# Attention products of a pair of heads: two runs for four on TensorE, and two 256-column fills in one PSUM bank

## The chip, the cores and the metric

The kernel runs on one core of one Trainium2 chip. The metric is the device time of one execution in microseconds (us). A core has five engines that work side by side, each through its own list of instructions in order: TensorE (PE, matrix products into the accumulator memory PSUM), VectorE (DVE), ScalarE (ACT), GpSimd (POOL) and SyncE (SP), which issues the transfers. One engine waits for another by semaphores that stand in front of an instruction; everything behind that instruction on the same engine waits with it. PSUM is used in banks of 512 float32 columns.

## The reference

Two results are computed from separate inputs and set side by side. The left half is attention in four segments of 512 rows with 32 heads of 18 features, with a memory that is carried from segment to segment; the right half is a two-dimensional Fourier transform written as products with given cosine and sine matrices.

```python
for s in range(N):                                   # N = 4 segments of L = 512, H = 32 heads
    qs, ks, vs = q[:, :, s], k[:, :, s], v[:, :, s]
    logits = jnp.einsum("bhqd,bhkd->bhqk", qs, ks) * scale + mask
    p = _softmax(logits, axis=-1)
    a_dot = jnp.einsum("bhqk,bhkd->bhqd", p, vs)
    ...
    outs.append(g * a_mem + (1.0 - g) * a_dot)
...
a = jnp.einsum("bsd,ed->bse", x, dft_hid_re)
b = jnp.einsum("bsd,ed->bse", x, dft_hid_im)
y = jnp.einsum("ts,bse->bte", dft_seq_re, a) - jnp.einsum("ts,bse->bte", dft_seq_im, b)
```

The sign of the mask is such that row i sees column j for j <= i, so of each 512 x 512 block of logits the kernel makes four row blocks of 128 rows with 128, 256, 384 and 512 columns.

## The kernel before

The program has three stages. From 0 to about 218 us the projections and the memory are made. From about 218 to 920 us two kinds of work share TensorE: the attention of 4 x 32 = 128 heads, and the transform, called the dense work. Behind that stands an output projection. The change lies in the middle stage.

**Dense work** (`hidden`, L620 on, and `sequence` and `product`, L642 and L580 on) is a long row of float32 products of 288 columns into the tiles `d` (L584 and L629 to L634). Each product has its own load of 128 x 128 weights (PEld in the profile), which can run beside the product ahead of it.

**Attention** (`attention`, L1155 on) runs in 68 passes, p = 0 to 67, over pairs of heads. Pass p holds steps of several pairs at once: the even head of pair p, the odd head of pair p - 2 (F_LAG = 2), the even head of pair p - 3 (T_LAG) and both heads of pair p - 4 (V_LAG). NP = 64 is the number of pairs. A pass is cut into eight slots, each ended by a `yield SLOTS[i]`. Behind each yield the main loop puts in dense work until its share has caught up with the attention's, so what stands between two yields goes to TensorE as one **run** of attention products, and dense products stand between the runs. The order on each engine is the order in which the program writes the instructions; there is no scheduler.

The steps that the change touches:

- `scores(n, kind)` multiplies queries and keys of head n into a bank tile `s` or `t` (L969). Kind 0 is the row block of 512 columns, kind 1 the blocks of 384 and 128 columns, kind 2 the block of 256 columns. `bank` hands out two `s` banks in turn, and two `t` banks.
- `smallest` (L975) adds the causal mask on DVE, writes the sum back into the bank and keeps the row minimum of the negated logits; each block is one such pass over the bank and a second, short instruction that reads the result out. DVE is free of a block only behind the second.
- `s_fill` is `scores` and `smallest` for an even head, whose minimum goes into `negm`; of it only the minimum is wanted. `f_fill` is the same for an odd head, with the minimum in `nb`; kind 0 takes a `t` bank. Its logits stay in the bank until `f_exp` (L995 and L998, on ACT) has taken their exponential into SBUF.
- `t_fill` makes the transposed logits of an even head (L1044 to L1054), `pv` the sums of probabilities and values of one head: 20 short products into the tile `pv` (L1093 and L1094). `pv_out` takes both heads' sums out on DVE. `f_turn` (L1014) is the transfer that transposes an odd head's probabilities before its `pv`; `maxima` (L1019 to L1022, POOL) splits the minima of two even heads for a later product.

Before the change a pass has four runs: A in slot 1 (`s_fill` 0, `t_fill` 0 and 1, `s_fill` 1), B in slot 3 (`pv` of the even head, `s_fill` 2), C in slot 4 (`f_fill` 1, `t_fill` 2, `f_fill` 0) and D in slot 6 (`pv` of the odd head, `f_fill` 2). In the text f1, f0, f2 stand for the products of `f_fill` 1, 0, 2 and s0, s1, s2 for those of `s_fill`.

Of the kernel before, what the change touches and what calls it, by code (L numbers as in the profile page):

```python
# [12 lines left out]
F32 = mybir.dt.float32  # L13
# [3 lines left out]
AF = mybir.ActivationFunctionType  # L17
# [5 lines left out]
S, D, H, DH, NSEG, L = 2048, 576, 32, 18, 4, 512  # L23
P = 128
# [16 lines left out]
def infini_attention_and_fnet(ctx: ExitStack, tc: tile.TileContext, xT, wqk, w8, wv, wo, beta, xtT, cT, hT, out):  # L41
    nc = tc.nc
    act, dve, pool, pe = nc.scalar, nc.vector, nc.gpsimd, nc.tensor
# [44 lines left out]
    def later(n, fn, *a):  # L88
        due.setdefault(clock[0] + n, []).append((fn, a))
# [374 lines left out]
    def stacks(p_, i):  # L464
        qs_bufs.append(p_.tile([P, 4, L], BF16, name=f"qs{i}"))
        ks_bufs.append(p_.tile([P, 4, L], BF16, name=f"ks{i}"))
        pool.memset(ks_bufs[i].bitcast(F32)[96:], BF16_ONES)
# [20 lines left out]
    def stack_load(G):  # L488
        if G < NG:
            s, g8 = divmod(G, 8)  # L490
            rows = slice(g8 * 72, g8 * 72 + 72)
            for n, (buf, src) in enumerate(((ks_bufs, kd), (qs_bufs, qd))):
                later(1 + n, dma, buf[G % 4][:NPAIR], src[s][rows].rearrange("(h d) c t -> (d c) h t", d=DH))
# [71 lines left out]
    def bank(name, shape, dtype, tag):  # L565
        turns[tag] ^= 1
        return ps.tile(shape, dtype, name=name, tag=f"{tag}{turns[tag]}", bufs=1)
# [392 lines left out]
    ROWS = (((3, 0),), ((0, 384), (2, 0)), ((1, 0),))  # L960
    FIRST_COL = {3: 0, 2: 512, 0: 896, 1: 1024}

    def scores(n, kind, tag="s"):
        G, h = divmod(n, 4)
        q, k = qs_bufs[G % 4][:NPAIR, h], ks_bufs[G % 4][:NPAIR, h]
        o = bank("s", [P, L], F32, tag)
        for i, c in ROWS[kind]:
            w = (i + 1) * P
            pe.matmul(o[:, c:c + w], q[:, i * P:w], k[:, :w], start=True, stop=True)  # L969
        return o  # L970
# [7 lines left out]
    def s_fill(n, kind):  # L978
        G, h = divmod(n, 4)
        smallest(scores(n, kind), kind, -1.0, NEGM[G % 2][:, 2 * h:2 * h + 4])  # L980
# [3 lines left out]
    def f_fill(n, kind):  # L984
        o = scores(n, kind, "s" if kind else "t")
        if kind == 1:
            F_[n] = [sa.tile([P, 4], F32, name="nb", bufs=2), sa.tile([P, 1280], F32, name="pf", bufs=3), {}]
        smallest(o, kind, -SCALE, F_[n][0])
        F_[n][2][kind] = o

    def f_exp(n, kind):
        nb, f, o = F_[n]
        o = o.pop(kind)
        m = nb[:, (slice(3, 4), slice(0, 3, 2), slice(1, 2))[kind]]
        act.activation(m, m, AF.Copy, bias=LIFT)  # L995
        for i, c in ROWS[kind]:
            w = (i + 1) * P
            act.activation(f[:, FIRST_COL[i]:FIRST_COL[i] + w], o[:, c:c + w], AF.Exp, bias=nb[:, i:i + 1], scale=-1.0)  # L998

    def f_split_hi(n):  # L1000
        f = F_[n][1]
# [14 lines left out]
    def maxima(G):  # L1016
        m, b = NEGM[G % 2].rearrange("p (h n) -> p h n", h=2), MB[G % 2][:, :24].rearrange("p (h c n) -> p c h n", h=2, c=3)
        r = sa.tile([P, 2, 4], F32, name="negx", bufs=2)
        pool.tensor_copy(b[:, 0], m)  # L1019
        pool.tensor_tensor(r, m, b[:, 0], OP.subtract)  # L1020
        pool.tensor_copy(b[:, 1], r)
        pool.tensor_tensor(b[:, 2], r, b[:, 1], OP.subtract)  # L1022

    def maxima_transpose(G, o):
        t = o[:, 384:512]
        pe.matmul(t, MB[G % 2], ident16, start=True, stop=True)
        yield
        w = sa.tile([24, P], BF16, name="mt", bufs=2)
        act.activation(w, t[:24], AF.Copy)
        for h in range(2):  # L1030
            later(1, dma, qs_bufs[G % 4][NPAIR:NPAIR + 3, 2 * h].rearrange("c (n t) -> c n t", n=4), w[12 * h:12 * h + 12])
# [64 lines left out]
    def pv_out(n2):  # L1096
        G, hh = divmod(n2, 2)
        s, g8 = divmod(G, 8)
        o = PV.pop(n2)
        og = OG[G % 2]  # L1100
        h0 = 4 * g8 + 2 * hh
        w = o[:, 440:].rearrange("p (h i c) -> p h i c", h=2, c=1)
        b = o[:, :144].rearrange("p (h i d) -> p h i d", h=2, i=4)
        o = o[:, :440].rearrange("p (h i c) -> p h i c", h=2, i=4)
        a = sa.tile([P, 8, DH], F32, name="pa", bufs=2)
        dve.reciprocal(w, o[:, :, :, 54:])
        dve.tensor_tensor(w, w, g1[:, h0:h0 + 2, None, None].to_broadcast([P, 2, 4, 1]), OP.mult)
        dve.tensor_reduce(a, o[:, :, :, :54].rearrange("p h i (c d) -> p (h i) d c", c=3), axis=AX, op=OP.add)
        to = og[:, :, 36 * hh:36 * hh + 36].rearrange("p i (h d) -> p h i d", d=DH)
        a = a.rearrange("p (h i) d -> p h i d", h=2)  # L1110
        if s == 0:
            dve.tensor_tensor(to, a, w.to_broadcast([P, 2, 4, DH]), OP.mult)
        else:
            dve.tensor_tensor(b, a, w.to_broadcast([P, 2, 4, DH]), OP.mult)
            dve.tensor_tensor(to, to, b, OP.add)
        if hh == 1:
            later(6, turn_out, G)
# [33 lines left out]
    F_LAG, T_LAG, V_LAG = 2, 3, 4  # L1151
    NP = 2 * NG
    SLOTS = (1060.0, 890.0, 1060.0, 660.0, 890.0, 1060.0, 650.0, 1210.0)

    def attention():  # L1155
        for p in range(NP + V_LAG):
            def even(lag, fn, *a):
                if 0 <= p - lag < NP:
                    fn(2 * (p - lag), *a)

            def odd(lag, fn, *a):
                if 0 <= p - lag < NP:
                    fn(2 * (p - lag) + 1, *a)

            if p < 2:
                OG.append(sa.tile([P, 4, 72], F32, name=f"og{p}"))
            if p == 0:
                stack_load(1)
                later(20, value_load, 0)
            if p % 2 == 0:  # L1170
                later(39, value_load, p // 2 + 1)
                later(30, memory_load, p // 2)
            even(T_LAG + 1, t_lo, 0)
            odd(F_LAG + 1, f_exp, 2)
            odd(F_LAG + 1, f_split_hi)
            yield SLOTS[0]
            G = p // 2 - 1 if p % 2 == 0 and 0 < p <= NP else None
            even(0, s_fill, 0)
            even(T_LAG, t_fill, 0)
            even(T_LAG, t_fill, 1, G)  # L1180
            even(0, s_fill, 1)
            if G is not None and p < T_LAG:
                list(maxima_transpose(G, bank("trm", [P, L], F32, "t")))
            odd(F_LAG + 1, f_split_lo, pool, 512, 1280)
            yield SLOTS[1]
            even(T_LAG, t_lo, 1)
            odd(F_LAG + 1, f_split_lo, dve, 0, 512)
            yield SLOTS[2]
            even(V_LAG, pv)
            if p < 2:  # L1190
                stacks(sq, p + 2)
            even(0, s_fill, 2)
            even(T_LAG, t_mask)
            yield SLOTS[3]
            odd(F_LAG, f_fill, 1)
            even(T_LAG, t_fill, 2)
            odd(F_LAG, f_fill, 0)
            if p % 2 and p < NP:
                maxima(p // 2)
            yield SLOTS[4]  # L1200
            odd(F_LAG + 1, f_turn)
            if p % 2:
                if p == 1:
                    later(6, stack_load, 2)
                else:
                    stack_load((p + 3) // 2)
                if 2 < p < 18:
                    later(2, copy_parts, 2, 7 + p // 2)
            elif 4 <= p < 36:
                later(2, copy_parts, 3, (p - 4) // 2)  # L1210
            even(T_LAG, t_hi)
            yield SLOTS[5]
            odd(V_LAG, pv)
            odd(F_LAG, f_fill, 2)
            odd(F_LAG, f_exp, 1)
            even(T_LAG, t_lo, 2)
            yield SLOTS[6]
            odd(F_LAG, f_exp, 0)
            if V_LAG <= p < NP + V_LAG - 1:
                pv_out(p - V_LAG)  # L1220
            yield SLOTS[7]
# [8 lines left out]
    for n, w in enumerate(attention()):  # L1230
        tick()
        ta += w
        for fn, a in PLAN.pop(n, ()):
            fn(*a)
        while td / total_d < ta / total_a:
            t = next(d, BREAK)
            if t is BREAK:
                break
            td += t
# [56 lines left out]
```

## Time and profile before

| what | value |
|---|---|
| median of three runs | 984.33 us (983.99 to 985.59) |
| the profiled execution's own time | 983.87 us |
| its span, first to last instruction | 982.2 us |
| TensorE products busy | 974.7 us (99%) |
| TensorE weight loads busy | 916.3 us (93%), beside the products |
| DVE, ACT, POOL busy | 746.6, 715.2, 664.4 us |
| granted TensorE clock, mean | 0.999 |

The page of the profile gives busy time by engine, and the chain of work that ended last. A timeline row gives start, duration, engine, line, operation, the tile written, the tiles read, the shape, how many equal instructions follow each other (x) and, in square brackets, idle time of the engine ahead of it with what ended it. Since products are pipelined, the recorded durations overlap; what a product costs TensorE is the distance from its start to the start of the one behind it. The first dense product behind a fill starts, in the records, some 0.03 us behind the fill's start, and the distance to the next one then holds the rest of the fill; so the cost of a run is read from its first start to the start of a dense product some places behind it, less what dense products cost there, for each dense product between.

### The profile page before, as it was taken

To read this page: it belongs to the slowest core of one execution; us is meant where nothing else is said; L and a number is where in the kernel's file an instruction comes from. 1 tells how busy PE (TensorE), PEld (TensorE's weight loads), DVE (VectorE), ACT (ScalarE), POOL (GpSimd) and SP (SyncE) were. 2 spreads that over 40 slices of the span, in tenths; PEclk is the share of its full clock that TensorE was granted. 3 is DMA by queue.
4 is the path that set the end of the run, shared out by engine and by line. 5 is a ranking of instruction groups with operands and counts; after the bars stand their busy time and mean duration, and the time that the engine had idled before them with its cause. 6 is when DMAs were issued, how large, how long until landed. Compare 5 with 4: busy or idle time off the path is not lost.

```text
span 982.2 us, 25421 instructions
## 1 busy us (share of the span) xinstructions
PE 974.7 (99%) x9246; PEld 916.3 (93%) x9246; DVE 746.6 (76%) x2113; ACT 715.2 (73%) x1687; POOL 664.4 (68%) x746
## 2 busy tenths in 40 slices
PE   9999999999999999999999999999999999999998
PEld 8989989899999999999999999999999999999998
DVE  6657668594677767777887777778888899988884
ACT  6757576664887787877878788887777877878442
POOL 2657577686667766676776776667677987776561
PEclk9999999999999999999999999999999999999999
DMA  7637557766877998999999997789999999997663
GB/s 240 200 118 242 199 171 252 238 239 182 191 183 209 219 239 233 216 210 254 233 243 241 235 210 191 184 203 217 242 238 252 242 237 240 233 207 184 173 203 109
DMA packets 304350, 209.96 MB, mean 214 GB/s; under 512 B 204992, under 2 KB 259136, under 8 KB 304192
## 3 DMA queue, kind: packets, MB, share of 16 engines
q1 hardware_dynamic: 304000, 208.20, 82.5%
q8 instruction: 72, 1.18, 0.5%
q14 instruction: 54, 0.44, 0.1%
q10 hardware_dynamic: 224, 0.14, 0.0%
HBM read 122.37 MB, written 58.98 MB: 185 GB/s over the span
## 4 chain that ended last, share of the span: by engine, by line
PE 98%; ACT 1%; DVE 1%; issue 0%
PE d L584 41%; PE s L969 7%; PE v L84 6%; PE qk L84 6%; PE qk L251 6%; PE pv L1093 4%; PE d L629 3%; PE d L630 3%; PE d L631 3%; PE t L869 2%; PE pv L1094 2%; PE d L869 2%; PE s L869 2%; PE m L364 1%; PE t L1044 1%; PE look L397 1%
## 5 line engine op out<-in xcount | busy, mean ns | idle before, releaser
L975 DVE CUSTOM_DVE_ANT_0 s<-s,causal 128x128 f32<-128x128 f32 (+3 forms) x512 | 250.1, 504 | 104.3 <-PE s L969 98.1
L457 POOL TENSOR_TENSOR clo<-craw,chi 128x512 fp32r<-128x512 f32 x159 | 217.6, 1369 | 97.1 <-ACT chi L452 72.2
L584 PE MATMUL d<-wide,chi 128*128 128x288 f32 x1408 | 260.1, 302 | 0.0
L584 PEld LDWEIGHTS d<-wide,chi 128*128 128x128 f32 x1408 | 210.5, 188 | 0.7
L584 PE MATMUL d<-wide,clo 128*128 128x288 f32 x704 | 171.2, 310 | 0.0
L1009 POOL TENSOR_TENSOR hl<-pf,hl 128x768 f16<-128x768 f32 x64 | 113.9, 1780 | 70.3 <-ACT hl L1005 56.1
L969 PE MATMUL s<-ks,qs 108*128 108x128 bf16 (+3 forms) x512 | 131.6, 301 | 1.9 <-ACT pf L998 1.8
L1057 ACT ACTIVATE phi<-t 128x384 f16<-128x384 f32 x128 | 61.7, 482 | 98.1 <-PE t L1054 98.1
L998 ACT ACTIVATE pf<-s,nb 128x128 f32<-128x128 f32 (+3 forms) x256 | 128.1, 526 | 6.2
L584 PE MATMUL d<-ab,chi 128*128 128x288 f32 x640 | 122.3, 300 | 0.0
L584 PEld LDWEIGHTS d<-wide,clo 128*128 128x128 f32 x704 | 117.7, 188 | 0.9
L452 ACT ACTIVATE chi<-craw 128x512 fp32r<-128x512 f32 x160 | 99.6, 623 | 2.8 <-DMA craw<-xtT 1.8
L584 PEld LDWEIGHTS d<-ab,chi 128*128 128x128 f32 x640 | 97.6, 188 | 0.3
L1005 ACT ACTIVATE hl<-pf 128x768 f16<-128x768 f32 (+1 forms) x128 | 87.4, 729 | 2.0
L584 PE MATMUL d<-ab,clo 128*128 128x288 f32 x320 | 82.4, 306 | 0.0
L629 PE MATMUL d<-wide,chi 128*128 128x288 f32 x256 | 79.7, 311 | 0.0
L630 PE MATMUL d<-wide,chi 128*128 128x288 f32 x256 | 75.6, 295 | 0.0
L631 PE MATMUL d<-wide,clo 128*128 128x288 f32 x256 | 75.6, 295 | 0.0
L1061 ACT ACTIVATE pf<-t 128x512 f32<-128x512 f32 (+1 forms) x128 | 68.7, 537 | 7.4 <-PE t L1044 7.3
L1076 POOL TENSOR_TENSOR plo<-pf,phi 128x384 f16<-128x384 f32 x64 | 60.7, 948 | 15.1 <-ACT pf L1061 12.6
L969 PEld LDWEIGHTS <-qs 108*128 108x128 bf16 x512 | 44.4, 97 | 16.3 <-issue 2.7
L289 POOL TENSOR_TENSOR p<-r,p 128x512 bf16<-128x512 f32 x36 | 43.4, 1206 | 22.3 <-ACT p L288 21.1
(286 smaller groups left out, 2596.6 us busy)
## 6 DMA issues: line engine op xcount, KB each, us to landing
craw<-cT SPq DMA_DIRECT2D x128, 256.0 KB
ks<-kd SPq DMA_DIRECT2D x32, 432.0 KB
qs<-qd SPq DMA_DIRECT2D x32, 432.0 KB
craw<-xtT SPq DMA_DIRECT2D x32, 320.0 KB
vd<-vs SPq DMA_DIRECT2D x16, 440.0 KB
vst<-vd SPq DMA_DIRECT2D x32, 220.0 KB
qd<-p SPq DMA_DIRECT2D x16, 384.0 KB
kd<-p SPq DMA_DIRECT2D x16, 384.0 KB
```

Source lines behind the costliest of these rows:

```text
L84: pe.matmul(o, a, b, start=n == 0, stop=n == len(terms) - 1)
L452: act.activation(hi, raw[:, :4], AF.Copy)
L457: engine.tensor_tensor(lo, raw[:, :4], hi.bitcast(F32), OP.subtract)
L584: pe.matmul(o[h], a, b[:, h * 288:h * 288 + 288], start=start, stop=stop)
L629: pe.matmul(o, xh[:, k], wl[k][:, cs], start=k == 0, stop=False)
L630: pe.matmul(o, xh[:, k], wh[k][:, cs], start=False, stop=False)
L631: pe.matmul(o, xl[:, k], wh[k][:, cs], start=False, stop=False)
L969: pe.matmul(o[:, c:c + w], q[:, i * P:w], k[:, :w], start=True, stop=True)
L975: dve.tensor_tensor_reduce(o[:, c:c + w], o[:, c:c + w], CAUSAL[0][:, L - w:], scale=scale, scalar=-LOWEST, op0=OP.add, op1=OP.min, accum_ ...
L998: act.activation(f[:, FIRST_COL[i]:FIRST_COL[i] + w], o[:, c:c + w], AF.Exp, bias=nb[:, i:i + 1], scale=-1.0)
L1005: act.activation(hl[:, 0, a:b], f[:, a:b], AF.Copy)
L1009: engine.tensor_tensor(hl[:, 1, a:b], f[:, a:b], hl[:, 0, a:b], OP.subtract)
```

## The change

`f_fill` 1, 0 and 2, `s_fill` 2, `t_fill` 2 and both `pv` of a pass move into one run at the end of slot 4; run A stays. `s_fill` 2 and the `f_fill` 2 of the same pass share one `s` bank: the first takes columns 0 to 255, the second columns 256 to 511 (the list `SHARED` hands the second half on). `f_exp` takes kinds 0 and 2 together and so lifts their two minima in one instruction instead of two. `maxima` moves behind the yield that ends slot 4.

```diff
     def scores(n, kind, tag="s"):
         ...
-        o = bank("s", [P, L], F32, tag)
+        if kind == 2 and SHARED:
+            o = SHARED.pop()
+        else:
+            o = bank("s", [P, L], F32, tag)
+            if kind == 2:
+                SHARED.append(o[:, 256:])
...
-    def f_exp(n, kind):
+    def f_exp(n, *kinds):
         nb, f, o = F_[n]
-        o = o.pop(kind)
-        m = nb[:, (slice(3, 4), slice(0, 3, 2), slice(1, 2))[kind]]
+        m = nb[:, 1 - kinds[0]::2]
         act.activation(m, m, AF.Copy, bias=LIFT)
-        for i, c in ROWS[kind]:
-            ...
+        for kind in kinds:
+            for i, c in ROWS[kind]:
+                ...
+            del o[kind]
...
-            odd(F_LAG + 1, f_exp, 2)
             odd(F_LAG + 1, f_split_hi)
             yield SLOTS[0]
...
             yield SLOTS[2]
-            even(V_LAG, pv)
             if p < 2:
                 stacks(sq, p + 2)
-            even(0, s_fill, 2)
             even(T_LAG, t_mask)
             yield SLOTS[3]
+            SHARED.clear()
             odd(F_LAG, f_fill, 1)
+            even(0, s_fill, 2)
             even(T_LAG, t_fill, 2)
             odd(F_LAG, f_fill, 0)
+            odd(F_LAG, f_fill, 2)
+            even(V_LAG, pv)
+            odd(V_LAG, pv)
+            yield SLOTS[4]
             if p % 2 and p < NP:
                 maxima(p // 2)
-            yield SLOTS[4]
...
             yield SLOTS[5]
-            odd(V_LAG, pv)
-            odd(F_LAG, f_fill, 2)
             odd(F_LAG, f_exp, 1)
             even(T_LAG, t_lo, 2)
             yield SLOTS[6]
-            odd(F_LAG, f_exp, 0)
+            odd(F_LAG, f_exp, 0, 2)
```

How the rows stand, in a pass in the middle of the program (names of tiles with their buffer numbers; a wait names the semaphore of the engine waited for). On TensorE before, the end of run B with s2 (tile s_8625), the dense products behind it, and run C with f1 (s_8641, two products) and f0 (s_8653):

```order
L969 MATMUL s_8625<-ks3_3055,qs3_3054 128x256 [waits DVE_49]
L584 MATMUL d_8348<-ab_3738,clo_8482 128x288
L584 MATMUL d_8349<-ab_3738,clo_8482 128x288
...
L969 MATMUL s_8641<-ks2_2920,qs2_2919 128x128 [waits DVE_49]
L969 LDWEIGHTS qs2_2919
L969 MATMUL s_8641<-ks2_2920,qs2_2919 128x384
...
L969 MATMUL s_8653<-ks2_2920,qs2_2919 128x512 [waits DVE_49]
...
L969 MATMUL s_8693<-ks2_2920,qs2_2919 128x256 [waits DVE_49]
L584 MATMUL d_8704<-wide_2869,chi_8580 128x288 [waits Activation_49]
```

The last fill, f2 (s_8693), closes run D and has dense products behind it. The bank of s_8693 is that of s_8625: two `s` banks go round, and s_8641 stands between (s_8653 is a `t` bank). Now, the one run that takes the place of B, C and D, from its second product (f1's block of 384 columns, s_8746) to the first weights of `pv`:

```order
L976 MATMUL s_8746<-ks2_2920,qs2_2919 128x384
L976 LDWEIGHTS qs3_3054
L976 MATMUL s_8753<-ks3_3055,qs3_3054 128x256 [waits DVE_49]
L1062 LDWEIGHTS ks2_2920
L1062 MATMUL t_8756<-qs2_2919,ks2_2920 128x128 [waits Activation_49]
L1063 LDWEIGHTS ks2_2920
L1063 MATMUL t_8756<-qs2_2919,ks2_2920 128x256
L976 LDWEIGHTS qs2_2919
L976 MATMUL s_8761<-ks2_2920,qs2_2919 128x512 [waits DVE_49]
L976 LDWEIGHTS qs2_2919
L976 MATMUL s_8753<-ks2_2920,qs2_2919 128x256 [waits DVE_49]
L1102 LDWEIGHTS phi_8500
```

s2 and f2 are the two products into s_8753, with t_fill 2 (t_8756) and f0 (s_8761) between them; behind f2 stand the 40 products of both `pv`. On DVE, the reductions of the same pass before, s2 (into negm1), f1 and f0 (into nb):

```order
L975 ISA s_8625,negm1_2424<-s_8625,causal_2421 128x256 [waits PE_49]
L975 ISA negm1_2424 128x1
L975 ISA s_8641,nb_8644<-s_8641,causal_2421 128x128 [waits DVE_49,PE_49]
L975 ISA nb_8644 128x1
L975 ISA s_8641,nb_8644<-s_8641,causal_2421 128x384 [waits DVE_49]
...
L975 ISA s_8653,nb_8644<-s_8653,causal_2421 128x512 [waits PE_49]
```

and now, with s2's behind f1's two and f2's last:

```order
L982 ISA s_8746,nb_8749<-s_8746,causal_2421 128x128 [waits PE_49]
L982 ISA nb_8749 128x1
L982 ISA s_8746,nb_8749<-s_8746,causal_2421 128x384 [waits DVE_49]
...
L982 ISA s_8753,negm1_2424<-s_8753,causal_2421 128x256 [waits PE_49]
L982 ISA negm1_2424 128x1
L982 ISA s_8761,nb_8749<-s_8761,causal_2421 128x512 [waits PE_49]
...
L982 ISA s_8753,nb_8749<-s_8753,causal_2421 128x256 [waits PE_49]
```

In the program as built, the DVE wait in front of f2 asks, before and now, for the count that DVE reaches with the read-out of s2's reduction (the second of the two rows that name negm1 above). Before, two stretches of dense work, run C and a `pv` lie between s2 and f2; now 896 columns of fills do. `s_fill` 2 and `f_fill` 2 meet in one bank in 62 of the passes (p = 2 to 63).

More of the change, by code (lines that the diff above doesn't have):

```diff
@@ L961, in infini_attention_and_fnet @@
     FIRST_COL = {3: 0, 2: 512, 0: 896, 1: 1024}
+    SHARED = []
     def scores(n, kind, tag="s"):
@@ L989, in f_fill @@
         F_[n][2][kind] = o
-    def f_exp(n, kind):
+    def f_exp(n, *kinds):
         nb, f, o = F_[n]
-        o = o.pop(kind)
-        m = nb[:, (slice(3, 4), slice(0, 3, 2), slice(1, 2))[kind]]
+        m = nb[:, 1 - kinds[0]::2]
         act.activation(m, m, AF.Copy, bias=LIFT)
-        for i, c in ROWS[kind]:
-            w = (i + 1) * P
-            act.activation(f[:, FIRST_COL[i]:FIRST_COL[i] + w], o[:, c:c + w], AF.Exp, bias=nb[:, i:i + 1], scale=-1.0)
+        for kind in kinds:
+            for i, c in ROWS[kind]:
+                w = (i + 1) * P
+                act.activation(f[:, FIRST_COL[i]:FIRST_COL[i] + w], o[kind][:, c:c + w], AF.Exp, bias=nb[:, i:i + 1],
+                               scale=-1.0)
+            del o[kind]
     def f_split_hi(n):
```

## The prediction

> **What bounds the kernel now.** I read the page's first part, then the chain of work that ended last, then the waits of TensorE.
>
> ```profile
> span 982.2 us, 25421 instructions
> PE 974.7 (99%) x9246; PEld 916.3 (93%) x9246; DVE 746.6 (76%) x2113; ACT 715.2 (73%) x1687; POOL 664.4 (68%) x746
> ...
> PE 98%; ACT 1%; DVE 1%; issue 0%
> ...
> PE s L969 <- ACT pf L998: 1.8, 4, 0.5
> ```
>
> TensorE sets the end: it is busy in 99% of the span, it makes 98% of the chain, and all that it waits for in the middle stage is four times ACT, 1.8 us together. Every microsecond by which an attention run grows or shrinks on TensorE therefore shows in full, and work taken off another engine shows nowhere. So the question is how long the one new run holds TensorE against runs B, C and D. One pass, read in the timeline of TensorE, gives the old price.
>
> ```profile
> 502.41 0.20 PE L1093 MATMUL pv<-vst,phi 128*128 128x55 bf16 x1
> ...
> 502.94 0.27 PE L969 MATMUL s<-ks,qs 108*128 108x256 bf16 x1
> 502.96 0.78 PE L584 MATMUL d<-wide,chi 128*128 128x288 f32 x4
> 503.58 0.39 PE L969 MATMUL s<-ks,qs 108*128 108x128 bf16 x2
> 503.81 0.22 PE L1053 MATMUL t<-qs,ks 111*128 111x128 bf16 x1
> 503.87 0.27 PE L1054 MATMUL t<-qs,ks 111*128 111x256 bf16 x1
> 503.98 0.38 PE L969 MATMUL s<-ks,qs 108*128 108x512 bf16 x1
> 504.01 0.62 PE L584 MATMUL d<-wide,clo 128*128 128x288 f32 x2
> 504.46 0.70 PE L584 MATMUL d<-wide,chi 128*128 128x288 f32 x4
> 505.00 0.43 PE L584 MATMUL d<-wide,clo 128*128 128x288 f32 x2
> 505.27 0.69 PE L584 MATMUL d<-wide,chi 128*128 128x288 f32 x4
> ```
>
> Six dense products go from 504.46 to 505.27, 0.135 us each. Run B starts at 502.41 and run C at 503.58, with four dense products between: 1.17 - 0.54 = **0.63 us** for B, of which 0.53 is the `pv` and 0.10 the fill s2. From 503.58 to 504.46 stand run C and two dense products: 0.88 - 0.27 = **0.61 us** for C; f0 starts 0.40 into it and so costs 0.21. Run D has B's form and is priced like it. B, C and D together: 0.63 + 0.61 + 0.63 = **1.87 us** a pass.
>
> **The new run, part by part.** (1) The products. None is added or dropped: f1, s2, t_fill 2 and f0 go out one behind another. With C's own 0.61 and 0.10 for s2, TensorE stands before f2 **0.71 us** after f1 began, if nothing holds it.
>
> (2) The hold in front of f2. f2 writes the other half of s2's bank and waits for the read-out of s2's reduction, which now stands third in DVE's queue, behind both of f1's. Here is what DVE does with run C now, and how a TensorE fill follows a DVE read-out that it waited for (the fill at 758.90, whose run met a busy DVE):
>
> ```profile
> 503.46 0.42 DVE L975 CUSTOM_DVE_ANT_0 s<-s,causal 128x256 f32<-128x256 f32 x1
> 503.81 0.13 DVE L975 DVE_READ_ACCUMULATOR2_ANT negm<- 128x1 f32 x1
> 504.01 0.30 DVE L975 CUSTOM_DVE_ANT_0 s<-s,causal 128x128 f32<-128x128 f32 x1
> 504.23 0.14 DVE L975 DVE_READ_ACCUMULATOR2_ANT nb<- 128x1 f32 x1
> 504.40 0.57 DVE L975 CUSTOM_DVE_ANT_0 s<-s,causal 128x384 f32<-128x384 f32 x1
> 504.89 0.14 DVE L975 DVE_READ_ACCUMULATOR2_ANT nb<- 128x1 f32 x1
> 504.89 0.73 DVE L975 CUSTOM_DVE_ANT_0 s<-s,causal 128x512 f32<-128x512 f32 x1
> ...
> 758.71 0.14 DVE L975 DVE_READ_ACCUMULATOR2_ANT negm<- 128x1 f32 x1
> 760.12 0.33 DVE L975 CUSTOM_DVE_ANT_0 s<-s,causal 128x128 f32<-128x128 f32 x1
> ...
> 758.90 0.38 PE L969 MATMUL s<-ks,qs 108*128 108x128 bf16 x2
> ```
>
> Run C's f1 starts at 503.58 and DVE takes it up at 504.01, 0.43 later. Its two reductions keep DVE until the next block starts at 504.89, 1.31 after f1. Now s2's reduction stands there: in its own row it starts at 503.46 and its read-out ends at 503.94, 0.48 later, so it would end at 1.31 + 0.48 = 1.79. The read-out that ended at 758.85 let TensorE start at 758.90, so 0.05 more: f2 starts **1.84 us** after f1, where TensorE was ready at 0.71. It stands for 1.13 us. TensorE takes its products in order, so the 40 `pv` products and all dense work queue behind this wait; nothing covers it. Before, the same wait cost nothing because run C, a `pv` and two stretches of dense work lay between s2 and f2.
>
> [...]
>
> (3) The rest of the run: f2 0.10, then two `pv`. The first costs 0.53. The second is followed by a dense product instead of a fill. The trace has such a run near the end, where fills have run out:
>
> ```profile
> 919.76 0.20 PE L1093 MATMUL pv<-vst,ptt 128*128 128x55 bf16 x1
> ...
> 920.27 0.18 PE L1094 MATMUL pv<-vst,ptt 128*128 128x37 bf16 x1
> 920.30 0.51 PE L584 MATMUL d<-wide,clo 128*128 128x288 f32 x2
> 920.64 0.70 PE L584 MATMUL d<-ab,chi 128*128 128x288 f32 x4
> ```
>
> From 919.76 to 920.64 it is 0.88 with two dense products, so 0.61 for a `pv` that ends a run: 0.08 over 0.53. The weights of the next dense product have no long fill to load beside any more. All four runs of a pass end in a fill before; now one of two doesn't.
>
> The new run: 1.84 + 0.10 + 0.53 + 0.61 = **3.08 us**, against 1.87: **+1.21 us a pass**. In 62 passes both fills stand in the bank: 62 x 1.21 = **+75 us**.
>
> (4) Fewer runs. If entering a run cost something, B and D would show it against their parts. C has 1408 columns; at s2's 0.10 us for 256 they would take 0.55, and it takes 0.61. So at most 0.06 an entry, 2 x 62 x 0.06 = 7 us gained at the highest, and nothing at the lowest, since an entry can't be told there from what five products cost beside one. I take nothing: the 0.10 is rounded, and 0.11 for s2 would leave nothing over in C.
>
> (5) DVE late with f1. DVE may still be at earlier work when f1 comes. In the run at 758.90 it took up f1 at 760.12, 1.22 later instead of 0.43, and the hold would grow by those 0.79. Against this stand the idle times ahead of its reductions:
>
> ```profile
> L975 DVE CUSTOM_DVE_ANT_0 s<-s,causal 128x128 f32<-128x128 f32 (+3 forms) x512 | 250.1, 504 | 104.3 <-PE s L969 98.1 <-ACT hl L1005 0.3
> L995 ACT ACTIVATE nb<-nb 128x1 f32<-128x1 f32 (+1 forms) x192 | 38.0, 198 | 1.9 <-DVE nb L975 1.5
> 448.55 0.38 PE L969 MATMUL s<-ks,qs 108*128 108x128 bf16 x2 [0.51 <-ACT pf L998]
> ```
>
> 104.3 us over 64 passes is 1.6 us a pass in which DVE waits, nearly always for TensorE, and the longer pass gives it 1.2 us more. A backlog can't last. Bounds: 0, and a quarter of the passes as late as that one, 62 x 0.25 x 0.79 = 12 us. I take a third of that, **+4 us**, nearer to the pass at 503.58.
>
> (6) Small parts. `f_exp` 2 leaves slot 0, directly ahead of run A; the four waits of TensorE for it (the row at 448.55 is one) go: **-2 us**. One lifting instruction of 198 ns per odd head goes from ACT, hidden behind TensorE; were ACT the bound, it would be 64 x 0.2 = 13 us. `maxima` moves back by one slot on POOL; its product stands in the next pass's run A, four slots of dense work later. `pv` of the odd head now comes sooner after the transposing transfer:
>
> ```profile
> L1093 PE MATMUL pv<-vst,ptt x640: 186/187/201, 268.2 to 920.2; 128*128 128x55 bf16 x160
> L1014 SPq DMA_TRANSPOSE ptt<-hl x64: 2982/3907/5730, 253.4 to 910.6; - x64
> ```
>
> From first to first it is 14.8 us and at the end 9.6 us from issue to use, with an issue of at most 5.7; the move is over one stretch of dense work, of which 504.01 to 505.27 is most, and the hold gives 1.1 us back. Nothing.
>
> Sum: 75 + 4 - 2 = +77 us on the span of 982.2, 1059. The median of the runs shown, 984.33, lies 2.1 above that span, so the forecast is **1061 us**. The unknowns: the links of DVE's chain to 0.1 us (6 us either way), the entries (7 down), the backlog (4 down, 8 up): 1047 to 1075 for this case.
>
> **The rivals.** *DVE falls behind.* Its reductions now come in one cluster of five blocks, 0.88 + 0.48 + 0.65 + 0.48 = 2.5 us in a row (504.01 to 504.89 for f1, 504.89 to 505.54 for f0's block), and with half of the passes as late as that at 758.90 the sum gains 62 x 0.5 x 0.79 = 24 us in place of 4: about 1081. For it speaks that DVE is busy for 76%; against it that the hold itself gives DVE time. Chance 0.07.
>
> ```profile
> 505.54 0.14 DVE L975 DVE_READ_ACCUMULATOR2_ANT nb<- 128x1 f32 x1
> ```
>
> *No hold.* The wait in front of f2 could be met by the time TensorE reaches it. Then the run costs 0.71 + 0.10 + 0.53 + 0.61 = 1.95, +0.08 a pass or +5 us, less 2 for run A, less up to 7 for the two entries: 980 to 987, at the middle 984, which is no change. It decides at one point: whether s2's read-out ends within 0.71 us of f1's start. DVE needs 0.43 before it even starts and has three blocks to do, so I give it 0.04.
>
> *The clock falls.* Each hold could let the granted clock drop for what follows. The trace has holds of 0.5 us (448.55) inside a stretch at full clock, and only in the last stretch, where TensorE is idle for 4 of 52 us, the clock reads less:
>
> ```profile
> 260.00:500.00 240.00, 238.53 (x2589) 224.98 (x2589) 181.72 (x575) 190.80 (x454) 162.86 (x182) 1.00 0.93 224
> 930.00:982.00 52.00, 47.83 (x362) 47.59 (x360) 35.73 (x72) 18.72 (x50) 23.00 (x31) 0.99 0.46 151
> ```
>
> Were the clock halved for the 1.24 us from f2 to the run's end, it would be 62 x 1.24 = 77 us more: 1138. [...] Chance 0.03.
>
> **How the numbers follow.** The likeliest case, the hold at about its worked size, has 0.86. The range 1046 to 1082 holds it and most of the late DVE, and leaves out the rivals without hold and with the lower clock. A difference of 0.2%, 2 us, is about what a measurement of this kernel can tell from no change. Slower: the three cases with a hold, 0.96, and 0.005 from the slow end of the case without: 0.965. The rest of that case is 0.02 faster and 0.015 the same.
>
> **What would show it.** In the changed kernel's waits, TensorE's fills wait for DVE's reductions about 62 times. The record counts idle time from the modelled end of f0, which lies 0.38 after its start at 0.50, so each shows as 1.84 - 0.88 = 0.96 and together as some 60 us. In the timeline f2 starts about 0.05 behind the read-out into negm. TensorE's busy time stays near 975 us while its share falls to about 93%; ACT has 64 fewer lifting instructions, and run A waits for nothing. I am wrong if f2 follows f0 at 0.2 us, if DVE takes up f1 much later than 0.43 in most passes, or if the clock in the middle stage falls below 1.00.

## The result, and the profile after

The changed kernel takes 1069.87 us (median; 1069.55 to 1070.24 in four runs) against 984.50 us before on the same chip. The ratio is 1.0867, with a 95% interval of 1.0854 to 1.0880: **slower by 85 us**, inside the predicted range and 9 us above the forecast. The profiled execution's span is 1067.8 us, 85.6 more than before.

The page of the changed kernel, busy times and the chain of work that ended last:

```profile
span 1067.8 us, 25263 instructions
PE 991.1 (93%) x9246; PEld 924.7 (87%) x9246; DVE 744.8 (70%) x2113; ACT 702.0 (66%) x1623; POOL 661.1 (62%) x746
...
PE 77%; DVE 13%; ACT 7%; issue 2%; DMA 1%; SPq 0%; POOL 0%; POOLq 0%
```

TensorE has the same 9246 products, but its share falls from 99% to 93%. The chain, which was TensorE for 98% before, now goes through DVE and ACT too. The waits of TensorE (total us, times, longest us) have one row of any size, and the row for ACT is gone:

```profile
PE s L976 <- DVE negm L982: 71.3, 62, 2.7
```

62 times, once in each pass in which the two fills share a bank. One such pass, first TensorE and then DVE in the timeline:

```profile
409.34 0.50 PE L976 MATMUL s<-ks,qs 108*128 108x128 bf16 x3
409.68 0.22 PE L1062 MATMUL t<-qs,ks 111*128 111x128 bf16 x1
409.74 0.27 PE L1063 MATMUL t<-qs,ks 111*128 111x256 bf16 x1
409.85 0.38 PE L976 MATMUL s<-ks,qs 108*128 108x512 bf16 x1
411.22 0.27 PE L976 MATMUL s<-ks,qs 108*128 108x256 bf16 x1 [1.00 <-DVE negm L982]
...
412.36 0.77 PE L584 MATMUL d<-ab,chi 128*128 128x288 f32 x4
412.97 0.43 PE L584 MATMUL d<-ab,clo 128*128 128x288 f32 x2
```

```profile
408.70 0.68 DVE L1018 TENSOR_TENSOR hl<-pf,hl 128x512 f16<-128x512 f32 x1
409.77 0.30 DVE L982 CUSTOM_DVE_ANT_0 s<-s,causal 128x128 f32<-128x128 f32 x1 [0.39 <-PE s L976]
...
410.16 0.57 DVE L982 CUSTOM_DVE_ANT_0 s<-s,causal 128x384 f32<-128x384 f32 x1
...
410.64 0.47 DVE L982 CUSTOM_DVE_ANT_0 s<-s,causal 128x256 f32<-128x256 f32 x1
411.02 0.14 DVE L982 DVE_READ_ACCUMULATOR2_ANT negm<- 128x1 f32 x1
411.02 0.73 DVE L982 CUSTOM_DVE_ANT_0 s<-s,causal 128x512 f32<-128x512 f32 x1
```

The run begins at 409.34 with f1 and s2 (the x3). DVE takes f1 up 0.43 later, goes through f1's two blocks and then s2's, whose read-out into `negm` ends at 411.02 + 0.14 = 411.16. TensorE's f2 starts at 411.22, 1.88 behind f1. f0 had started at 409.85 and costs 0.21, so TensorE was ready at 410.06 and stood for 1.16 us; the record shows 1.00 of that, because it counts from f0's modelled end. From f2 to 412.97 it is 1.75 with four dense products, so 1.21 for f2, both value sums and the end of the run. The run holds TensorE for 1.88 + 1.21 = 3.09 us.

### The profile page after: what moved, and what is told of

Same layout as the page of the kernel before. It is cut to its first block, busy times and chain, and to the rows that moved or that the text cites. A ratio compares the mean times of both kernels' runs of the same rounds, so it can differ in the third digit from the quotient of the medians.

```text
span 1067.8 us, 25263 instructions
## 1 busy us (share of the span) xinstructions
PE 991.1 (93%) x9246; PEld 924.7 (87%) x9246; DVE 744.8 (70%) x2113; ACT 702.0 (66%) x1623; POOL 661.1 (62%) x746
## 4 chain that ended last, share of the span: by engine, by line
PE 77%; DVE 13%; ACT 7%; issue 2%; DMA 1%; SPq 0%; POOL 0%; POOLq 0%
PE d L584 33%; DVE s L982 7%; PE v L84 6%; PE qk L84 6%; PE qk L251 5%; PE s L976 4%; PE pv L1102 4%; PE t L869 2%; PE pv L1103 2%; PE d L629 2%; PE d L631 2%; PE d L630 2%; DVE hl L1018 2%; ACT pf L1005 2%; ACT hl L1014 1%
## 5 line engine op out<-in xcount | busy, mean ns | idle before, releaser
L982 DVE CUSTOM_DVE_ANT_0 s<-s,causal 128x128 f32<-128x128 f32 (+3 forms) x512 | 244.8, 512 | 130.8 <-PE s L976 125.8
L457 POOL TENSOR_TENSOR clo<-craw,chi 128x512 fp32r<-128x512 f32 x159 | 222.5, 1399 | 160.3 <-ACT chi L452 126.3
L584 PE MATMUL d<-wide,chi 128*128 128x288 f32 x1408 | 257.2, 300 | 0.0
L976 PE MATMUL s<-ks,qs 108*128 108x128 bf16 (+3 forms) x512 | 122.6, 302 | 71.3 <-DVE negm L982 71.3
L584 PE MATMUL d<-wide,clo 128*128 128x288 f32 x704 | 167.0, 304 | 0.0
L1018 POOL TENSOR_TENSOR hl<-pf,hl 128x768 f16<-128x768 f32 x64 | 109.7, 1714 | 59.8 <-ACT hl L1014 45.8
L1005 ACT ACTIVATE pf<-s,nb 128x128 f32<-128x128 f32 (+3 forms) x256 | 121.1, 524 | 4.2
L584 PE MATMUL d<-ab,chi 128*128 128x288 f32 x640 | 120.1, 297 | 0.0
L1102 PEld LDWEIGHTS <-phi 128*128 128x128 f16 x640 | 38.3, 96 | 85.6 <-issue 85.2
L629 PE MATMUL d<-wide,chi 128*128 128x288 f32 x256 | 77.3, 302 | 0.0
L630 PE MATMUL d<-wide,chi 128*128 128x288 f32 x256 | 75.6, 295 | 0.0
L631 PE MATMUL d<-wide,clo 128*128 128x288 f32 x256 | 75.5, 295 | 0.0
L1085 DVE TENSOR_TENSOR plo<-pf,phi 128x512 f16<-128x512 f32 x64 | 59.5, 929 | 1.9 <-ACT phi L1079 1.9
```

Source lines behind the costliest of these rows:

```text
L457: engine.tensor_tensor(lo, raw[:, :4], hi.bitcast(F32), OP.subtract)
L584: pe.matmul(o[h], a, b[:, h * 288:h * 288 + 288], start=start, stop=stop)
L629: pe.matmul(o, xh[:, k], wl[k][:, cs], start=k == 0, stop=False)
L630: pe.matmul(o, xh[:, k], wh[k][:, cs], start=False, stop=False)
L982: dve.tensor_tensor_reduce(o[:, c:c + w], o[:, c:c + w], CAUSAL[0][:, L - w:], scale=scale, scalar=-LOWEST, op0=OP.add, op1=OP.min, accum_ ...
L1005: act.activation(f[:, FIRST_COL[i]:FIRST_COL[i] + w], o[kind][:, c:c + w], AF.Exp, bias=nb[:, i:i + 1], scale=-1.0)
```

## The experiments

In each row "before" is the kernel before on the same chip. The results, in us; the expectations stand below.

| kernel | time | before | ratio, 95% interval |
|---|---|---|---|
| changed | 1069.87 | 984.50 | 1.0867 (1.0854 to 1.0880) |
| both fills first | 985.42 | 984.85 | 1.0006 (0.9997 to 1.0015) |
| both fills first, f0 last | 980.38 | 984.85 | 0.9948 (0.9935 to 0.9961) |
| f2 apart | 987.22 | 984.85 | 1.0020 (1.0010 to 1.0029) |
| s2 first | 1009.30 | 984.85 | 1.0242 (1.0225 to 1.0258) |
| s2 late | 1143.93 | 984.64 | 1.1629 (1.1584 to 1.1673) |
| f2 last | 999.90 | 984.64 | 1.0154 (1.0137 to 1.0171) |
| f_exp merged alone | 982.54 | 984.78 | 0.9979 (0.9971 to 0.9988) |
| f0 last, f_exp split | 983.13 | 984.78 | 0.9983 (0.9974 to 0.9992) |

### Both fills first: the bank and the run stay, the wait goes

The two new steps issue the products of s2 and f2 into the two halves of the bank; `s_fill` 2 and `f_fill` 2 then only reduce them. The two steps themselves are left out here.

```diff
...
             odd(F_LAG, f_fill, 1)
+            even(0, s_scores)
+            odd(F_LAG, f_scores)
             even(0, s_fill, 2)
             even(T_LAG, t_fill, 2)
             odd(F_LAG, f_fill, 0)
             odd(F_LAG, f_fill, 2)
             even(V_LAG, pv)
             odd(V_LAG, pv)
```

> The one run, the shared bank and DVE's order of reductions stay; only f2 is filled directly behind s2, ahead of s2's reduction, so that TensorE has nothing to wait for between the two fills. Theory of the hold (TensorE stands in front of f2 until s2's read-out, 1.88 us behind f1): the hold goes, f2 starts 0.33 us behind f1, the run costs some 1.96 us against 1.89 for B, C and D, and the time is about 987 us (984 to 990). Rival, the cluster of five reductions on DVE is the cost wherever TensorE meets it: TensorE waits for DVE in run A or at f1 instead, and the time stays above 1040. Rival, the merged run itself (two value sums in a row) is the cost: above 1040 too, with no waits.

985.42 us, and no wait of TensorE in the middle stage. Its timeline, one run (the x4 are f1, s2 and f2):

```profile
410.68 0.61 PE L976 MATMUL s<-ks,qs 108*128 108x128 bf16 x4
411.13 0.22 PE L1071 MATMUL t<-qs,ks 111*128 111x128 bf16 x1
...
411.30 0.38 PE L976 MATMUL s<-ks,qs 108*128 108x512 bf16 x1
412.55 0.51 PE L584 MATMUL d<-wide,chi 128*128 128x288 f32 x2
412.89 0.29 PE L584 MATMUL d<-wide,clo 128*128 128x288 f32 x1
```

From 410.68 to 412.89 with two dense products: 2.21 - 0.27 = 1.94 us, as expected. Same bank, same products, same order of DVE's reductions and the same two value sums in a row: moving one 256-column product ahead of one reduction (and so ahead of t_fill 2 and f0 too) takes the whole loss away. Both rivals fall: neither DVE's cluster of reductions nor the merged run costs anything like 85 us.

### Both fills first, f0 last: what the end of the run costs

```diff
-            odd(F_LAG, f_fill, 0)
             odd(F_LAG, f_fill, 2)
             even(V_LAG, pv)
             odd(V_LAG, pv)
+            odd(F_LAG, f_fill, 0)
```

> As the kernel with both fills first, but f0 (512 columns) is filled behind the two value sums, so that the run ends in a long fill. Theory of the exposed weights (a value sum that ends a run costs 0.08 us more, since the next dense weights have nothing long to load beside): 62 x 0.08 = 5 us less than the kernel with both fills first, some 982 us (980 to 985). Rival, the end of the run does not matter: the same time as that kernel, within 1 us.

980.38 us, 5.0 less than the kernel above, where 5 were expected. Its run in the timeline:

```profile
409.69 0.61 PE L976 MATMUL s<-ks,qs 108*128 108x128 bf16 x4
...
411.34 0.38 PE L976 MATMUL s<-ks,qs 108*128 108x512 bf16 x1
411.37 0.62 PE L584 MATMUL d<-wide,chi 128*128 128x288 f32 x2
411.82 0.30 PE L584 MATMUL d<-wide,clo 128*128 128x288 f32 x1
```

From 409.69 to 411.82 with two dense products: 2.13 - 0.27 = 1.86 us. Over all such runs of the trace the mean is 1.88 us against 1.96 with the value sums at the end. In the kernel above the second dense product behind the value sums starts at 412.76, 0.21 behind the first, where dense products stand 0.13 apart. In the changed kernel's run above it starts at 412.58, 0.22 behind the first, and its weights load only from 412.45 to 412.64, right behind the first's (412.34 to 412.53). So the 0.08 us are read as the weights' there. This kernel is faster than the kernel above and than the kernel before.

### f2 apart: the bank is shared, the fills are not close

```diff
             odd(F_LAG, f_fill, 0)
-            odd(F_LAG, f_fill, 2)
             even(V_LAG, pv)
             odd(V_LAG, pv)
...
             yield SLOTS[5]
+            odd(F_LAG, f_fill, 2)
             odd(F_LAG, f_exp, 1)
```

> The shared bank stays, but f2 goes back to its old place in slot 6 as a run of its own, behind a stretch of dense work. Theory of the hold: sharing costs nothing when s2's read-out is over by then; no wait in front of f2; two value sums still end a run (+0.08 us a pass) and f2 is one run more: about 987 us (984 to 991). Rival, two fills in one bank cost by themselves, wherever they stand: above 1040.

987.22 us, as expected, with no wait in front of f2. So sharing the bank cost nothing by itself here, where s2's read-out was over by the time TensorE came to f2.

### s2 first, and s2 late: the size of the hold

Two orders of the same steps. First:

```diff
+            even(0, s_fill, 2)
             odd(F_LAG, f_fill, 1)
-            even(0, s_fill, 2)
             even(T_LAG, t_fill, 2)
             odd(F_LAG, f_fill, 0)
             odd(F_LAG, f_fill, 2)
```

> Only the order of s2 and f1 changes in the one run: s2 and its reduction come first. Theory of the hold, by its size: DVE takes up s2 some 0.31 us behind its fill (as f2's in run D before, 506.59 to 506.90), reads out 0.49 later, and 0.05 more lets f2 start at 0.85 us where TensorE is ready at 0.71: a hold of 0.14 instead of 1.17 us, and with the late DVE of some passes (0.15 on average) some 0.3. The time is about 1002 us (996 to 1010). Rival, the hold does not depend on what DVE does between: the same 1070 as the changed kernel.

1009.30 us, at the upper end of what was expected. The run's median over the trace is 2.09 us: the 0.85 of the expectation and 1.24 from f2 to the run's end. Its mean is 2.27, so DVE's lateness adds 0.18 us on average where 0.15 was expected. That is 2 us of the 7 by which 1002 was missed; the rest lies in the expectation's own sum, since a hold of 0.3 us on top of the 987 us expected without one gives 987 + 62 x 0.3 = 1006. TensorE's waits:

```profile
PE s L976 <- DVE negm L982: 11.1, 21, 1.7
PE s L976 <- ACT pf L1005: 1.4, 4, 0.5
```

The second row is a side effect: in this order the first fill of run A (the one at 403.75, for example) waits in four passes for ACT to finish the merged `f_exp`.

Then:

```diff
             odd(F_LAG, f_fill, 1)
-            even(0, s_fill, 2)
             even(T_LAG, t_fill, 2)
             odd(F_LAG, f_fill, 0)
+            even(0, s_fill, 2)
             odd(F_LAG, f_fill, 2)
```

> The other way: s2 and its reduction come behind f0's, so one block of 512 columns more (0.65 us) stands ahead of s2's read-out on DVE, and f2 is filled directly behind s2. Theory of the hold: f2 starts 1.31 + 0.65 + 0.48 + 0.05 = 2.49 us behind f1 against 1.88, 62 x 0.61 = 38 us more than the changed kernel: about 1108 us (1100 to 1116). Rival, the hold does not depend on DVE's order: the same 1070.

1143.93 us: far over the expected 1108, though the way was right. The wait itself has the expected size:

```profile
PE s L976 <- DVE negm L982: 110.6, 62, 3.3
```

110.6 - 71.3 = 39 us more than in the changed kernel, where 38 were expected. The profiled execution, the longest of four, has a span of 1150.1 us, 82 us more than the changed kernel's 1067.8; so some 43 us of it have another cause (at the median it is 35). The busy times by stretches (TensorE's clock is the number behind POOL's) show it:

```profile
280.00:540.00 260.00, 225.59 (x2236) 211.00 (x2235) 159.62 (x499) 163.62 (x374) 144.41 (x160) 0.93 0.70 176
...
300.40:303.80 3.40, 1.54 (x13) 1.10 (x12) 3.00 (x10) 2.57 (x7) 3.02 (x4) 1.00 0.51 160
303.80:307.20 3.40, 3.04 (x46) 2.98 (x46) 2.15 (x9) 3.04 (x9) 1.27 (x1) 0.50 1.19 194
```

```profile
304.15 0.37 PE L976 MATMUL s<-ks,qs 108*128 108x256 bf16 x1 [2.21 <-DVE negm L982]
305.93 0.83 PE L584 MATMUL d<-wide,chi 128*128 128x288 f32 x2
```

The hold of 2.21 us ends at 304.15. In the 3.4 us up to 303.80 TensorE was busy for only 1.54, and in the next 3.4 us it is granted half its clock. The trace has 30 such windows of 3.41 us at half clock in the attention stage. At most 30 x 3.41 / 2 = 51 us can be lost in them, less where TensorE stands anyway, against 3 us in the changed kernel's two; the 43 us fit. The four executions bear it out. Their spans are 1138.9, 1141.9, 1142.5 and 1150.1 us, and their mean granted clocks 0.964, 0.961, 0.961 and 0.955; span times the missing share of the clock is 41, 45, 45 and 52 us, and without it all four come to 1097 to 1098 us. No run took the clock apart from the wait.

### f2 last: the wait under cover

```diff
             odd(F_LAG, f_fill, 0)
-            odd(F_LAG, f_fill, 2)
             even(V_LAG, pv)
             odd(V_LAG, pv)
+            odd(F_LAG, f_fill, 2)
```

> The two value sums go out between f0 and f2, so that they cover the wait and f2 ends the run. Theory of the hold: TensorE comes to f2 at 0.71 + 1.06 = 1.77 us, s2's read-out allows it at 1.88, and with the late DVE of some passes at 2.03 on average: a hold of 0.1 to 0.26 us, no exposed weights: 990 to 1000 us. Rival, the hold is fixed at some 1.1 us wherever f2 stands: about 1065.

999.90 us, the upper end. The wait row reads 10.9 us in 18 passes instead of 71.3 in 62:

```profile
PE s L976 <- DVE negm L982: 10.9, 18, 1.7
```

The two value sums (1.06 us) cover all but some 0.1 us of the steady hold: the run's median is 1.99 us, against 1.86 for the run without a wait that ends in f0. What the wait row shows are the passes in which DVE is late; with them the mean is 2.14.

### The two small parts alone

The kernel before, with `f_exp` of kinds 0 and 2 merged in slot 6, and nothing else; `f_exp` itself is written as in the change:

```diff
...
-            odd(F_LAG + 1, f_exp, 2)
             odd(F_LAG + 1, f_split_hi)
...
-            odd(F_LAG, f_exp, 0)
+            odd(F_LAG, f_exp, 0, 2)
```

> The kernel before with one part of the change alone: f_exp takes kinds 0 and 2 together in slot 6, so that the exponential of f2's block no longer stands directly ahead of run A; runs B, C and D stay. Theory of run A's waits: TensorE's four waits for ACT, 1.8 us, go, and the time falls by about 2 us (982 to 984). Rival, the merge is worth nothing on TensorE's path: the time of the kernel before within 0.7 us. Rival, ACT now waits in slot 6 for f2's reduction and holds back dense work behind it: slower by more than 1 us.

982.54 us, 2.2 less than before. In its trace TensorE's four waits for ACT are gone, and their 1.8 us lie within the interval of the gain. And the reverse, the fastest kernel without this part, with `f_exp` as in the kernel before:

```diff
...
+            odd(F_LAG + 1, f_exp, 2)
             odd(F_LAG + 1, f_split_hi)
...
-            odd(F_LAG, f_exp, 0, 2)
+            odd(F_LAG, f_exp, 0)
```

> The kernel with both fills first and f0 at the run's end, but with f_exp of kind 2 back in slot 0 as in the kernel before. It tells what the two runs for four are worth alone: at the same run cost (1.88 us against 1.89 for B, C and D) and with run A's waits back, theory says the time of the kernel before, 983 to 985 us. Rival, fewer runs save something that the runs' own times do not show: still about 980.5 us.

983.13 us, 1.7 less than before, in the expected range; the rival's 980.5 falls. So the 4.5 us of the fastest kernel fall into 2.2 for the merged `f_exp` and about 2 for two runs instead of four. The trace of this last kernel has the four waits for ACT again (1.5 us), and its run takes 1.87 us on average against 1.89 for B, C and D, which is some 1 us in 62 passes. The rest of those 2 us is within the intervals and has no cause shown.

## Why the prediction was right, and where its sizes were off

**The hold in front of f2 (part 2)** was right in kind and size. 62 waits were forecast and 62 stand there; f2 starts 1.88 us behind f1 where 1.84 was worked out from the rows before, and in the median of the 62 passes DVE takes f1 up 0.43 us behind its start, as forecast. Removing the wait, with the bank, the products and DVE's order as they were, brought the time back to 985.42, and moving s2 forward, moving it back or covering the wait changed the loss in the way and, for the waits, by the size that DVE's queue gives. How the time would be with this order and without the wait was not tried, since the wait can't be taken away alone. Nor did a run give f2 a bank of its own; that the wait is there because of the bank is read from the built program.

**The end of the run (part 3)**: 0.08 us a pass were taken from the one place in the old trace where a value sum ended a run. The two kernels that differ in whether f0 stands ahead of the value sums or behind them are 5.0 us apart, 62 x 0.08.

**Steady sum**: 3.09 against 1.87 us, +1.22 a pass and 76 us, where 75 were forecast. One sign came otherwise: TensorE's busy time was to stay near 975 us and is 991.1. The record counts the first 0.16 us of each hold as busy (1.00 recorded of 1.16), 62 x 0.16 = 10 us, and the run's end adds 62 x 0.08 = 5.

**DVE late with f1 (part 5)** is the term that was mis-sized: 4 us forecast, about 9 measured. The wait row's 71.3 us over 62 passes are 1.15 on average, 0.15 over the steady 1.00. The argument was that a backlog on DVE can't last, since the longer pass gives DVE time. What delays f1 is not a backlog of that kind but single pieces of DVE work that stand just ahead of f1's reduction. In 20 passes the recorded hold is over 1.05 us, together 9.3 us over the steady 1.00, and in each of them the row of DVE directly ahead of f1's reduction is the subtraction of L1018 or a step that reads the dense tiles (L94, L654). The worst pass, DVE and then TensorE:

```profile
855.65 1.58 DVE L1018 TENSOR_TENSOR hl<-pf,hl 128x512 f16<-128x512 f32 x1
857.15 0.44 DVE L654 TENSOR_TENSOR y<-y,d 128x288 f32<-128x288 f32 x1
857.51 0.29 DVE L982 CUSTOM_DVE_ANT_0 s<-s,causal 128x128 f32<-128x128 f32 x1
```

```profile
855.41 0.50 PE L976 MATMUL s<-ks,qs 108*128 108x128 bf16 x3
...
858.96 0.27 PE L976 MATMUL s<-ks,qs 108*128 108x256 bf16 x1 [2.66 <-DVE negm L982]
```

The run starts at 855.41, but DVE is held by a subtraction that takes 1.58 us here and 0.68 in the pass at 408.70, and by a dense output, and takes f1 up 2.10 later. When that subtraction began, POOL was in an instruction of L457:

```profile
855.41 1.27 POOL L457 TENSOR_TENSOR clo<-craw,chi 128x512 fp32r<-128x512 f32 x1 [2.33 <-ACT chi L452]
```

POOL's ends at 856.68 and DVE's at 857.23, 0.55 later. The five longest of the 64 such subtractions on DVE in this trace, 1.30 to 1.72 us, all began while POOL was in L457, and each ends 0.55 us behind POOL's; most of the others take 0.68 us. The one at 752.23 began while POOL was in L457 too (752.22 to 754.03), but took 0.67 us. So that POOL holds DVE in the five was not shown, and no run moved POOL's work.

**The clock (third rival)**, given 0.03 as a whole case as the author's estimate beside holds of 0.5 us at full clock, was a small part of the truth: two windows of half clock follow the longest hold, 2.66 us, and the third longest, 1.86 us.

```profile
260.00:855.00 595.00, 540.39 (x5721) 504.16 (x5721) 414.55 (x1312) 414.90 (x967) 370.30 (x421) 1.00 0.80 201
860.30:863.70 3.40, 3.40 (x16) 3.40 (x16) 2.46 (x7) 2.39 (x4) 2.89 (x2) 0.50 0.98 228
942.20:945.60 3.40, 3.40 (x32) 3.40 (x29) 2.85 (x9) 2.75 (x6) 3.36 (x4) 0.50 1.08 200
```

They cost at most 2 x 3.4 / 2 = 3.4 us. All terms: 76 + 9 + 3 - 2 = 86 us, against 85.6 in the spans.

**Fewer runs (part 4)** were taken at nothing with 7 us as the upper bound; the measured 2 us lie low between. **Run A's waits (part 6)**: 2 us forecast, 2.2 measured with that part alone.

## What to carry to other kernels

In this program the second fill of a shared PSUM bank waits for the reader of the first (1.16 us in a steady pass of the changed kernel). Issue both fills before the first reduction (985.42 us against 1069.87), or leave as much other work between them as the reading engine needs for its whole queue up to that reduction (987.22). Merging runs on an engine that is busy for 99% saved some 2 us here; what decided was the wait and the end of the run, so let a run of short products end in a long one (5 us here). And work out a hold from the queue of the engine that ends it, with its late passes, not from the one reduction.

## What the hardware showed that was not expected

In the changed kernel a pause of TensorE of 2.66 us and one of 1.86 us were each followed by 3.41 us at half clock, from 860.28 and from 942.20 us on; these two starts lie 81.92 us apart, 24 times the recorded 3.413. Cut into windows of this length that fit the recorded clock changes, the traces of the changed kernel and of the one with s2 late had the clock halved for exactly one window after each of the 14 windows in which TensorE's recorded idle time was over 1.75 us; of 33 windows between 1.64 and 1.74 us 18 were followed by a slow window, and of those with 1.60 us or less none was. The length of the pause alone does not sort them: the changed kernel's hold of 2.02 us, which ends at 823.53, is split by these windows into 1.22 and 0.80 us and has no slow window behind it, while the shorter one of 1.86 us has one. In the changed kernel the 42 holds that stay near the steady 1.00 recorded us have none behind them either. With s2 late, where the 62 holds are 1.78 recorded us on average (110.6 in all), 30 slow windows stand in the attention stage, and their price is about as large as the wait's growth: some 43 us beside 39 in the profiled execution.
